# Regrouping the early weight loads of a SwiGLU feed-forward kernel, and the order of its first matmuls

## The chip, the cores and the metric

The kernel runs on one core of one Trainium2 chip. The metric is the device time of one execution in microseconds (us); lower is better. Where one number stands for a kernel it is the median of several executions.

## The reference

All inputs and the output are bf16. There are 2048 tokens, D is 512 and F is 1376.

```python
B, S, D, F = 1, 2048, 512, 1376
def reference(x, w_gate, w_up, w_down):
    g = _silu(x @ w_gate)
    u = x @ w_up
    return (g * u) @ w_down
```

## The kernel before

The kernel computes h = silu(x @ w_gate) * (x @ w_up) with F on the partitions, tile by tile of 128 columns of F, and then multiplies h by w_down. F is 10 full tiles and a rest of 96 columns. The tokens run in 4 chunks of 512 for the first part. For each chunk and F tile there is a *gate* group and an *up* group; a group is 4 matmuls (D is 4 blocks of 128) that add up in one bank of PSUM, 128 x 512 in fp32. ScalarE (ACT) applies silu to the gate's bank and VectorE (DVE) multiplies the result with the up's bank into `hT_sb` (lines 281 and 288). There are 8 banks, used in turn, so groups 0 to 7 (gates and ups of F tiles 0 to 3 of the first chunk: even numbers are gates, odd numbers ups) need no bank to come free. The rest of 96 columns has groups of its own (lines 377 and 388), and the second matrix product follows from line 426 on; the change touches neither.

The engines run without a common clock; each has its own list of instructions, and waits on semaphores. A load has a semaphore of its own that reaches 16 when it has landed, and TensorE (PE) waits for it once, at the first matmul that needs the load (`need`).

*Loads.* Weights are loaded in *slabs*, runs of F tiles, the gates of a slab in one DMA and the ups in another. Each DMA writes 128 partitions with 4 rows each (one for each block of D), a row being 256 bytes per F tile. `slabs` lists the runs as pairs (first tile, tile after the last), and `slab_of` gives the slab's first tile for each tile, which is the name PE waits on. SyncE (SP) issues most loads, in the order written in `loads_on_sync`: token tile 0 (`xn0`), gate 0, then gate and up of tile 1, gates and ups of tiles 2 and 3, two transposing loads of tokens 256 to 383 and 384 to 511 (`x0b`, `x0c`), the two later slabs, the rest of w_up, the other three chunks of x by transposing loads, and w_down. ScalarE's queue issues token tile 1 and up 0 at the start. GpSimd issues no load.

*The start of PE.* PE first runs 10 matmuls on constants (line 338), then transposes the first 256 tokens itself (line 349; DVE and ACT copy the result to `xT_sb`). With these 256 tokens it then runs the first halves (columns 0 to 255) of groups 0 to 7, in an order written out by hand; group 0 in two pieces of 128 columns. Then it runs the second halves in the order of the groups, group 0 again in two pieces, of which the first waits for `x0b` and the second for `x0c`. From group 8 on a group runs over all 512 tokens at once. All these matmuls are issued on line 329, in `gu_matmuls`:

```python
need(("wg" if g["kind"] == "G" else "wu") + str(slab_of[ft]))
```

Of the kernel before, what the change touches and what calls it, by code (L numbers as in the profile page):

```python
# [13 lines left out]
def bass_standalone__swiglu_ffn__prompt_kernel(nc, x, w_gate, w_up, w_down, out):  # L14
# [5 lines left out]
    NFT = NFF + 1  # L20
# [28 lines left out]
    with ExitStack() as es:  # L49
# [32 lines left out]
        def load_sem(name):  # L82
            loads[name] = sem(f"s_{name}")
            return loads[name]
# [6 lines left out]
        def load_x(eng, name, t0, t1):  # L91
            eng.dma_start_transpose(
                xT_sb[:, :, t0:t1], xf[t0:t1, :]
            ).then_inc(load_sem(name), 16)

        def load_w(eng, name, src, base, f0, f1):
            eng.dma_start(  # L97
                w_sb[:, :, base + f0:base + f1],
                src[:, f0:f1].rearrange("(k p) f -> p k f", p=P),
            ).then_inc(load_sem(name), 16)  # L100

        slabs = [(0, 1), (1, 2), (2, 4), (4, 7), (7, NFT)]
        slab_of = {ft: a for a, b in slabs for ft in range(a, b)}

        def load_gate(eng, a, b):
            load_w(eng, f"wg{a}", w_gate, 0, a * P, min(b * P, F))

        def load_up(eng, a, b):
            load_w(eng, f"wu{a}", w_up, UPH, a * P, min(b * P, F - 32))

        def load_xn(eng, i):
            eng.dma_start(xn_sb[:, i, :], xf[i * P:(i + 1) * P, :]).then_inc(load_sem(f"xn{i}"), 16)  # L112
# [5 lines left out]
        def loads_on_sync(sp):  # L118
            load_xn(sp, 0)
            load_gate(sp, *slabs[0])  # L120
            for a, b in slabs[1:3]:
                load_gate(sp, a, b)
                load_up(sp, a, b)
            load_x(sp, "x0b", HT, HT + P)
            load_x(sp, "x0c", HT + P, SC)
            for a, b in slabs[3:]:
                load_gate(sp, a, b)
                load_up(sp, a, b)
            load_w(sp, "wut", w_up, F - (F - 32), F - 32, F)
            for c in range(1, NSC):  # L130
                load_x(sp, f"x{c}", c * SC, (c + 1) * SC)
            sp.dma_start(
                wd_sb[:, 0:NFF, :], w_down[0:NFF * P, :].rearrange("(k p) d -> p k d", p=P)
            ).then_inc(load_sem("wd"), 16)
            load_sem("wdt")
            for y0 in (0, 64):
                sp.dma_start(wd_sb[y0:y0 + 64, T01, :], w_down[NFF * P:F - SR, :]).then_inc(loads["wdt"], 16)
            for x0 in range(0, P, SR):
                sp.dma_start(wd_sb[x0:x0 + SR, T2, :], w_down[F - SR:F, :]).then_inc(loads["wdt"], 16)
            sp.dma_start(wd_sb[0:F_LAST, TAIL, :], w_down[NFF * P:F, :]).then_inc(load_sem("wdl"), 16)  # L140
# [109 lines left out]
        def on_sync(sp):  # L250
            loads_on_sync(sp)
            for t, c0, c1, ob, eng, n in stores:
                sp.wait_ge(s_A if eng == "A" else s_D, n)
                sp.dma_start(of[t * P:(t + 1) * P, c0:c1], o_sb[ob][:, c0:c1]).then_inc(s_out[ob], 16)
            for i in range(NOS):
                sp.wait_ge(s_out[i], 16 * n_store[i])
# [38 lines left out]
        def on_tensor(pe):  # L295
# [19 lines left out]
            def gu_matmuls(g, n0, n1):  # L315
                c, ft = g["c"], g["ft"]
                if c > 0:
                    need(f"x{c}")
                if c == 0 and n1 > HT:
                    need("x0b")  # L320
                if c == 0 and n1 > HT + P:
                    need("x0c")
                need(("wg" if g["kind"] == "G" else "wu") + str(slab_of[ft]))
                col = (0 if g["kind"] == "G" else UPH) + ft * P
                for dk in range(KD):
                    if c == 0 and dk % 2 == 0:
                        for i in range(n0 // P, min(n1 // P, NXN)):
                            after(*xt_ready[i, dk // 2])
                    ins = pe.matmul(  # L329
                        g["bank"][:, n0:n1], lhsT=w_sb[:, dk, col:col + P],  # L330
                        rhs=xT_sb[:, dk, c * SC + n0:c * SC + n1], start=(dk == 0), stop=(dk == KD - 1),
                    )
                if n1 == SC:
                    ins.then_inc(s_P, 1)
# [22 lines left out]
            first = groups[0:NB]  # L357
            for n0, n1 in ((0, P), (P, HT)):
                gu_matmuls(first[0], n0, n1)
            for at in (1, 2, 3, 4, 6, 5, 7):  # L360
                gu_matmuls(first[at], 0, HT)
            for n0, n1 in ((HT, HT + P), (HT + P, SC)):
                gu_matmuls(first[0], n0, n1)
# [108 lines left out]
        on_gpsimd(nc.gpsimd)  # L472
        on_scalar(nc.scalar)
        on_tensor(nc.tensor)
        on_vector(nc.vector)

# [27 lines left out]
```

## Time and profile before

| what | us |
|---|---|
| runs shown | 120.72, 119.93, 120.71 |
| their median | 120.71 |
| the profiled execution, its device time | 120.27 |
| its span, first to last instruction | 119.0 |
| PE busy | 115.6 |
| DVE busy / ACT busy | 37.7 / 34.8 |

The profile is of one execution. PE are the matmuls, PEld the weight loads that go ahead of them, DVE and ACT the vector and the scalar engine, SPq the queue of SP. A line of the chain of work has a start, a length and what ran. A line of the waits names who waited, for whom, the total, the number of waits and the longest. A line of the DMA issues has destination and source, the queue, how many, KB each and the time from issue to landing. A line of a table by stretches has the stretch, its length, then for PE, PEld, DVE, ACT and POOL the busy time and (x) the number of instructions, then the granted clock of PE, the busy share of the DMA engines and what they moved in GB/s. L329 is line 329 of the kernel.

### The profile page before, as it was taken

How to read it: one execution, taken by the hardware profiler on the slowest of the kernel's cores; microseconds unless marked ns; L12 is line 12 of the kernel's file. 1: busy time of each engine (PE TensorE's matmuls, PEld its weight loads, DVE VectorE, ACT ScalarE, POOL GpSimd, SP SyncE). 2: the span in 40 equal slices, each digit the busy share in tenths (PEclk: the TensorE clock that was granted, in tenths of full speed). 3: DMA queues.
4: the chain of work that ended last, by engine and by line, in shares of the span. 5: the costliest groups of instructions: out<-in, count | busy, mean ns of one | idle time of the engine just before them, and what ended most of it. 6: DMA issues, size and time to landing. Idle time of an engine off the chain costs nothing.

```text
span 119.0 us, 2293 instructions
## 1 busy us (share of the span) xinstructions
PE 115.6 (97%) x993; PEld 59.6 (50%) x1001; DVE 37.7 (32%) x57; ACT 34.8 (29%) x60; POOL 1.1 (1%) x7
## 2 busy tenths in 40 slices
PE   7999999999999999999999999999999999999993
PEld 2778444444444444444444444444444445885452
DVE  0105633444434444334444344360000044003320
ACT  4306334362343272442363432430000033003021
POOL 1000000000000000000000000000000000000000
PEclk9999999999999999999999999999999999999999
DMA  2999999992000000000000000000000017200252
GB/s 78 277 190 330 311 165 216 237 357 59 0 6 0 0 0 0 0 0 6 0 0 6 0 0 0 0 0 6 0 6 0 0 59 238 67 0 0 83 187 88
DMA packets 17643, 8.83 MB, mean 74 GB/s; under 512 B 10625, under 2 KB 17633, under 8 KB 17633
## 3 DMA queue, kind: packets, MB, share of 16 engines
q1 hardware_dynamic: 16960, 8.42, 27.5%
q10 hardware_dynamic: 672, 0.26, 0.8%
q8 instruction: 8, 0.13, 0.5%
q14 instruction: 3, 0.02, 0.0%
HBM read 4.75 MB, written 2.10 MB: 58 GB/s over the span
## 4 chain that ended last, share of the span: by engine, by line
PE 92%; DMA 3%; SPq 2%; issue 1%; DVE 0%
PE bank L329 57%; PE bank L426 25%; PE bank L465 7%; DMA w_sb<-in_w_gate_dram 3%; PE bank L377 3%; PE bank L388 2%; SPq L97 1%; SPq L112 0%; DVE o_sb L292 0%
## 5 line engine op out<-in xcount | busy, mean ns | idle before, releaser
L329 PE MATMUL bank<-xT_sb,w_sb 128*128 128x512 bf16 (+2 forms) x355 | 70.0, 355 | 0.4
L329 PEld LDWEIGHTS bank<-xT_sb,w_sb 128*128 128x128 bf16 x360 | 34.2, 98 | 35.3 <-DMA w_sb<-in_w_gate_dram 0.4
L288 DVE TENSOR_TENSOR hT_sb<-sg_sb,bank 128x512 bf16<-128x512 f32 x40 | 27.5, 687 | 40.8 <-PE bank L329 34.5
L281 ACT ACTIVATE sg_sb<-bank 128x512 f32<-128x512 f32 x40 | 23.8, 596 | 41.2 <-PE bank L329 41.2
L426 PE MATMUL bank<-wd_sb,hT_sb 32*128 32x512 bf16 x496 | 29.0, 374 | 0.0
L426 PEld LDWEIGHTS bank<-wd_sb,hT_sb 32*128 32x128 bf16 x496 | 15.3, 93 | 11.5 <-issue 0.4
L292 DVE CAST o_sb<-bank 128x512 bf16<-128x512 f32 (+1 forms) x9 | 5.5, 643 | 31.3 <-PE bank L426 25.9
L281 ACT ACTIVATE o_sb<-bank 128x512 bf16<-128x512 f32 (+1 forms) x8 | 4.3, 582 | 33.6 <-PE bank L426 27.9
L465 PE MATMUL bank<-wd_sb,hT_sb 128*128 128x512 bf16 (+2 forms) x45 | 7.8, 333 | 0.2 <-issue 0.2
L465 PEld LDWEIGHTS bank<-wd_sb,hT_sb 128*128 128x128 bf16 x46 | 4.1, 98 | 4.2 <-issue 0.4
L426 PE MATMUL bank<-wd_sb,hy_sb 32*128 32x512 bf16 (+1 forms) x32 | 5.0, 371 | 0.0
L377 PE MATMUL bank<-xT_sb,w_sb 128*128 128x512 bf16 x14 | 3.8, 379 | 0.1
L288 DVE TENSOR_TENSOR hx_sb<-sgx_sb,bank 32x512 bf16<-32x512 f32 x4 | 2.8, 692 | 3.5 <-ACT sgx_sb L281 3.5
L281 ACT ACTIVATE sgx_sb<-bank 32x512 f32<-32x512 f32 x4 | 2.3, 587 | 4.5 <-PE bank L377 4.5
L338 PE MATMUL bank<-const-bfloat16-1.0 128*128 128x512 bf16 (+1 forms) x10 | 2.8, 466 | 0.8 <-PEq L489 0.8
L426 PE MATMUL bank<-wd_sb,hx_sb 32*128 32x512 bf16 (+1 forms) x16 | 3.0, 371 | 0.0
L377 PEld LDWEIGHTS bank<-xT_sb,w_sb 128*128 128x128 bf16 x16 | 1.6, 98 | 1.9
L281 ACT ACTIVATE sgy_sb<-bank 64x512 f32<-64x512 f32 x4 | 2.4, 590 | 0.1
L338 PEld LDWEIGHTS bank<-const-bfloat16-1.0 128*128 128x128 bf16 x10 | 1.2, 139 | 2.2 <-issue 2.2
L388 PE MATMUL bank<-xT_sb,w_sb 128*64 128x512 bf16 x16 | 1.9, 382 | 0.0
L426 PEld LDWEIGHTS bank<-wd_sb,hy_sb 32*128 32x128 bf16 x32 | 1.6, 93 | 0.6
L292 DVE COPY xT_sb<-bank 128x256 bf16<-128x256 bf16 x2 | 0.6, 292 | 4.1 <-PE bank L349 4.0
(17 smaller groups left out, 8.3 us busy)
## 6 DMA issues: line engine op xcount, KB each, us to landing
out_dram<-o_sb SPq DMA_DIRECT2D x15, 128.0 KB, 1.8
wd_sb<-in_w_down_dram SPq DMA_DIRECT2D x1, 1280.0 KB, 7.4
w_sb<-in_w_gate_dram SPq DMA_DIRECT2D x1, 480.0 KB, 5.4
w_sb<-in_w_up_dram SPq DMA_DIRECT2D x1, 448.0 KB, 6.0
w_sb<-in_w_gate_dram SPq DMA_DIRECT2D x1, 384.0 KB, 3.8
w_sb<-in_w_up_dram SPq DMA_DIRECT2D x1, 384.0 KB, 4.6
w_sb<-in_w_gate_dram SPq DMA_DIRECT2D x2, 128.0 KB, 3.4
w_sb<-in_w_gate_dram SPq DMA_DIRECT2D x1, 256.0 KB, 3.9
```

Of the source, the lines that this page charges most:

```text
L97: eng.dma_start(w_sb[:, :, base + f0:base + f1], src[:, f0:f1].rearrange("(k p) f -> p k f", p=P),).then_inc(load_sem(name), 16)
L281: act.activation(op["out"], op["src"], fn).then_inc(s_A, 1)
L288: ins = dve.tensor_tensor(op["out"], op["a"], op["b"], ALU.mult)
L292: ins = dve.tensor_copy(op["out"], op["src"])
L329: ins = pe.matmul(g["bank"][:, n0:n1], lhsT=w_sb[:, dk, col:col + P], rhs=xT_sb[:, dk, c * SC + n0:c * SC + n1], start=(dk == 0), stop=(dk ...
L338: pe.matmul(banks[NB - 1][:, 0:width], lhsT=ones_w, rhs=ones_m[:, 0:width], start=True, stop=True)
L377: ins = pe.matmul(g["bank"][:, :], lhsT=w_sb[:, dk, XC0:XC0 + P], rhs=xT_sb[:, dk, c * SC:(c + 1) * SC], start=(dk == 0), stop=(dk == KD - 1),
L388: ins = pe.matmul(g["bank"][y0:y1, :], lhsT=w_sb[:, dk, YC0:YC0 + 64], rhs=xT_sb[:, dk, c * SC:(c + 1) * SC], start=(dk == 0), stop=(dk == ...
L426: ins = pe.matmul(g["bank"][:, 0:c1 - c0], lhsT=h, rhs=wd_sb[r0:r0 + SR, w, c0:c1], start=(start and fk == fks[0]), stop=(stop and fk == f ...
L465: ins = pe.matmul(g["bank"][:, 0:c1 - c0], lhsT=h, rhs=w, start=(last and fk == 0), stop=(fk == (NFF if last else NFF - 1)), skip_group_ch ...
```

## The change

Tile 1 and tiles 2 and 3 were two slabs and become one, tiles 1 to 3. Their gates are one load of 384 KB in rows of 768 bytes, and their ups another; before they were a gate load and an up load of 128 KB in rows of 256 bytes, and a gate load and an up load of 256 KB in rows of 512 bytes. SP issues two DMAs less ahead of the two transposing loads. The first halves of the groups run in the order gate 0, up 0, gates 1, 2, 3, ups 1, 2, 3; before it was gate 0, up 0, gate 1, up 1, gates 2, 3, ups 2, 3. The second halves keep their order, and so do all later loads.

```diff
-        slabs = [(0, 1), (1, 2), (2, 4), (4, 7), (7, NFT)]
+        slabs = [(0, 1), (1, 4), (4, 7), (7, NFT)]
...
             load_gate(sp, *slabs[0])
-            for a, b in slabs[1:3]:
-                load_gate(sp, a, b)
-                load_up(sp, a, b)
+            load_gate(sp, *slabs[1])
+            load_up(sp, *slabs[1])
             load_x(sp, "x0b", HT, HT + P)
             load_x(sp, "x0c", HT + P, SC)
-            for a, b in slabs[3:]:
+            for a, b in slabs[2:]:
                 load_gate(sp, a, b)
                 load_up(sp, a, b)
...
-            for at in (1, 2, 3, 4, 6, 5, 7):
+            for at in (1, 2, 4, 6, 3, 5, 7):
                 gu_matmuls(first[at], 0, HT)
```

## The prediction

> **What bounds the kernel now.** I read the page first: span, the busy shares, the slices.
>
> ```profile
> span 119.0 us, 2293 instructions
> PE 115.6 (97%) x993; PEld 59.6 (50%) x1001; DVE 37.7 (32%) x57; ACT 34.8 (29%) x60; POOL 1.1 (1%) x7
> PE   7999999999999999999999999999999999999993
> PE 92%; DMA 3%; SPq 2%; issue 1%; DVE 0%
> ```
>
> The tensor engine is busy for 97% of the span, and the chain that ended last lies on it for 92%. Nothing in the change alters the number or the shape of matmuls, so only the small part of the chain that is not PE can move. Next I read the chain of work in order of time, to find that part.
>
> ```profile
> 1.73 0.50 SPq L97
> 2.27 0.51 SPq L97
> 2.82 3.92 DMA w_sb<-in_w_gate_dram
> 6.74 0.05 issue
> 6.78 5.42 PE bank L329 x52
> ```
>
> Columns: start, length (us), what. The chain runs over the queue of SP into one load, the gates of F tiles 2 and 3, which lands at 2.82 + 3.92 = 6.74 us; from 6.78 on PE runs without a hole. So whatever moves the end of the first 256 tokens moves the end of the kernel by as much. The waits of PE's weight loads before 24 us, the only ones on a DMA:
>
> ```profile
> PEld bank L329 <- DMA w_sb<-in_w_gate_dram: 0.4, 1, 0.4
> PEld bank L329 <- DMA w_sb<-in_w_up_dram: 0.2, 1, 0.2
> ```
>
> Two short waits: up 1 (its weight loads begin at 6.04 us) and gate 2 (at 6.78 us). Last the issues of the DMAs, by narrow stretches, for size and time from issue to landing; the issue times are from the timeline of SP.
>
> ```profile
> 1.26 0.97 SPq L97 DMA_DIRECT2D w_sb<-in_w_gate_dram  x2
> 3.93 2.85 SPq L92 DMA_TRANSPOSE xT_sb<-in_x_dram  x2
> w_sb<-in_w_gate_dram SPq DMA_DIRECT2D x1, 128.0 KB, 3.8
> w_sb<-in_w_up_dram SPq DMA_DIRECT2D x1, 128.0 KB, 3.7
> w_sb<-in_w_gate_dram SPq DMA_DIRECT2D x1, 256.0 KB, 3.9
> w_sb<-in_w_up_dram SPq DMA_DIRECT2D x1, 256.0 KB, 4.2
> w_sb<-in_w_gate_dram SPq DMA_DIRECT2D x1, 384.0 KB, 3.8
> w_sb<-in_w_up_dram SPq DMA_DIRECT2D x1, 384.0 KB, 4.6
> ```
>
> Landings now: gate 1 at 1.73 + 3.8 = 5.53, up 1 at 2.27 + 3.7 = 5.97, gates 2-3 at 6.74, ups 2-3 at 3.37 + 4.2 = 7.57 us. And what the 16 DMA engines moved meanwhile (last column, GB/s):
>
> ```profile
> 3.00:4.00 1.00, 1.00 (x10) 0.80 (x9) 0.00 (x0) 0.23 (x2) 0.00 (x0) 1.00 1.25 287
> 4.50:5.00 0.50, 0.50 (x7) 0.34 (x8) 0.20 (x1) 0.41 (x2) 0.00 (x0) 1.00 0.98 188
> 5.00:5.50 0.50, 0.50 (x8) 0.38 (x6) 0.00 (x0) 0.00 (x0) 0.00 (x0) 1.00 1.11 294
> 5.50:6.75 1.25, 1.16 (x10) 0.62 (x8) 0.00 (x0) 0.00 (x0) 0.00 (x0) 1.00 1.16 340
> 10.00:12.00 2.00, 2.00 (x21) 1.79 (x19) 1.63 (x3) 1.39 (x3) 0.00 (x0) 1.00 1.03 342
> ```
>
> 287 GB/s while rows of 256 bytes are loaded, a dip to 188, then 340 in rows of 512 and 342 in rows of 768 and more.
>
> **The change, part by part.**
>
> *PE's pace.* The 52 matmuls of the chain from 6.78 us are 44 of 256 columns and 8 of 128, as much as 48 of 256: 5.42 us less some 0.16 for the last one's own length (273 ns against its step) is 0.11 us each, 0.44 us for a half group (4 matmuls). Gate 2 to up 3 are four half groups, so the second half of gate 0 starts at 6.78 + 1.76 = 8.54 us. Gate 1 starts at 5.55. Without any wait its six half groups (gates and ups 1 to 3) would end at 5.55 + 2.64 = 8.19. So the waits cost 0.35 us, which is all that can be won (0.3% of the time).
>
> *The waits, new.* The order is now gates 1, 2, 3, ups 1, 2, 3, and the first of them waits for all 384 KB of gates. If these land at L, gate 1 starts at L + 0.04 (as 6.74 to 6.78) and the six half groups end at L + 2.68. That equals 8.54 at L = 5.86. Each 0.1 us of L is 0.1 us of the kernel. What is queued behind: everything of PE, since it runs in order; ScalarE and VectorE have nothing from PE before the second halves (the first silu starts at 9.19 us), and shift with it.
>
> *L from below:* the 384 KB of gates that the kernel loads already took 3.8 us: 1.73 + 3.8 = 5.53, no wait at all. *From above:* by the landing of gates 2-3 now, 6.74, the queue has carried all that the new L needs and up 1 besides. *Between:* gate 1 lands at 5.53 now; 256 KB (262 kB) more at 340 GB/s are 0.77 us, so 6.30. The other way: from 6.74 take up 1's 131 kB, which went at a mean of 241 GB/s (188 and 294), 0.54 us: 6.20; if the dip goes too (half a us at 188 instead of 340: 0.22), 5.98; gate 1 in rows of 768 bytes at 340 instead of 287 saves 0.07: 5.91. The nearest rows give 5.9 to 6.3; I take 6.0, as fewer and larger transfers should do without most of the dip. Gate 1 then starts at 6.04, and the first halves end at 8.68: +0.14 us. A wait of 0.49 us (5.55 to 6.04) at gate 1 stands in the place of the 0.35 lost now.
>
> The Trainium skill (DMA: Bandwidth & Descriptors, Why a DMA increments its semaphore by 16 and not by 1) says that only the full count of 16 means that a load has landed, whatever part is there earlier. The trace agrees: up 1's weight loads start at 6.04, when that load is complete at 5.97, and no earlier. By this rule the merge holds gate 1 back for gates 2 and 3, and the sum is as above; were gate 1 free at its own third, it would start at 5.57 as now and 0.35 us would be won.
>
> *Ups.* Up 1 is needed at 6.04 + 3 x 0.44 = 7.36. Their 384 KB are the last bytes of the same total as now, after the gates: 6.0 + 393 kB / 340 GB/s = 7.16, hidden by 0.2 us. From below 2.27 + 4.6 = 6.87; from above 7.57, the landing of ups 2-3 now, when up 1 starts at 7.61 and the half groups end at 8.93: +0.39 us.
>
> *SP's queue.* Two issues less: 0.51 + 0.52 us and their gaps, 1.1 us, less 0.1 if an issue of 384 KB takes longer (0.58 us against 0.50). So the transposes of tokens 256 to 511 and all later loads are issued 1.0 us earlier. Now the transposes land at 3.93 + 4.3 = 8.23 and 5.52 + 3.1 = 8.62 us and are needed at 8.54 and 8.76: slack 0.31 and 0.14. Their data follows the ups: at the latest they land when they do now, and even a win of 0.35 would want the second at 8.41. Cost nothing at L = 6.0, and they cap a win at 0.14 us should they not come earlier at all. The gates of tiles 4 to 6 land at 6.82 + 3.8 = 10.62 for use at 12.26; covered by more. ACT's and POOL's queues are not touched.
>
> **Sum.** +0.14 us on the profiled execution's 120.27 us (span 119.0 and 1.3 around it): 120.4. The median of the runs shown is 0.44 higher, 120.71, which would give 120.85. The four times known (119.93, 120.27, 120.71, 120.72) have a mean of 120.4, so 120.55; I forecast 120.6.
>
> **Rivals.**
>
> *A, the forecast:* L of 5.8 to 6.4; one wait at gate 1 in place of two; -0.1 to +0.5 us.
>
> *B, the waits go:* gates land at 5.53, as the row of 3.8 us has it; gate 1 starts at 5.57, as now: -0.33 us, about 120.1 (from 120.4). For it: equal total bytes, fewer packets, and one 384 KB load that did take 3.8. Against it: that load had the DMA engines almost free (106 GB/s from 7.50 to 9.00), while this one has four others ahead of it. The Trainium skill (DMA: Bandwidth & Descriptors, Rules for kernel authors and Anatomy of one DMA) advises to coalesce small transfers and fits 2.0 us and bytes / 436e3 to a GpSimd-issued DMA: an estimate of 2.9 us for 384 KB, so a landing at 4.63 and no wait; no row here is as short for one of that size.
>
> *C, slower:* the gates land near 6.74, because the dip stays and the slowest of the 16 engines decides for a longer load: gate 1 starts at up to 6.78, the end moves to 9.42: +0.88 us, 121.3. It decides from L = 6.4 on. For it: the last loads landed 3.8 to 4.2 us after issue whatever their size, and three times the bytes queued at once may cost more. Against it: 131 kB less are ahead.
>
> *D, the ups end last:* +0.39 us at 7.57, 120.8; it needs the ups as late as 7.32 at L = 6.0. For it: the transposes follow directly behind them, as they do behind ups 2-3 now.
>
> *E, the clock:* the first five matmuls of 512 columns took 622 ns each, later ones 379; were PE to fall back to that pace during a wait, the 24 matmuls behind it (2.64 us) would take 622/379 as long, 1.7 us more, over 1% slower. Against it: behind the 0.4 us wait the matmuls still take 273 ns, and the new one is of the same kind.
>
> **How the numbers follow.** Chances: A 0.57, B 0.17, C 0.16, D 0.06, E 0.04. Executions differ by up to 0.8 us, so about 1% (1.2 us) is what a measurement tells from no change. The range reaches to B less some 0.2 of that scatter, 119.9, and to C with as much, 121.5. Faster by over 1% is out of reach of the 0.35 us and left to scatter, 0.03; slower by over 1% needs E or C at its worst with scatter, 0.08; the rest, 0.89, lies within 1%.
>
> **What would show it.** In the waits of PE's weight loads: one on the gate load of about 0.5 us with gate 1's weight loads from about 6.0, none or under 0.1 on the up load, and the long PE piece of the chain from there. A wait on gates under 0.1 is B; over 0.9 is C; one on ups of 0.2 or more is D; matmuls of 256 columns well over 273 ns after the wait are E. The rate from 4.5 to 5.0 us near 340 instead of 188 shows that the dip was one of many small loads. The forecast is wrong if the end of the first halves is not within 8.45 to 9.05 us, or if PE shows a new hole behind it.

## The result, and the profile after

| | before | after |
|---|---|---|
| median, 20 executions each (us) | 120.31 | 120.83 |
| lowest and highest | 119.93, 121.26 | 120.51, 123.48 |
| the profiled execution, device time | 120.27 | 120.63 |
| its span | 119.0 | 119.3 |

The changed kernel is slower: ratio 1.0051, 95% interval 1.0033 to 1.0068, or 0.4 to 0.8 us. The ratio leaves out one execution, of 123.48 with a granted clock of 0.986, the figure of the similar execution e15 below. It is a price of the change all the same: none of the 101 executions of the kernel before, in five batches, took more than 121.26. The changed kernel itself was timed many times in this one batch only.

The page of the changed kernel, the lines that were read first before:

```profile
span 119.3 us, 2299 instructions
PE 115.7 (97%) x1001; PEld 59.6 (50%) x1001; DVE 37.6 (32%) x57; ACT 34.9 (29%) x60; POOL 1.1 (1%) x7
```

PE does what it did; the loss is not in its work. (The traces lack a few matmul records, hence x993 before.) The chain in order of time (start, us, what):

```profile
1.25 4.38 DMA w_sb<-in_w_up_dram
5.62 0.05 issue
5.67 17.21 PE bank L328 x112
```

The waits of PE's weight loads before 24 us, and where the two last of them end (the timeline of PEld; the bracket is the idle time and what ended it):

```profile
PEld bank L328 <- DMA w_sb<-in_w_up_dram: 0.9, 1, 0.9
PEld bank L328 <- DMA w_sb<-in_w_gate_dram: 0.5, 2, 0.3
```

```profile
5.67 0.33 PEld L328 LDWEIGHTS bank<-xT_sb,w_sb 128*128 128x128 bf16 x4 [0.91 <-DMA w_sb<-in_w_up_dram]
6.22 0.11 PEld L328 LDWEIGHTS bank<-xT_sb,w_sb 128*128 128x128 bf16 x2 [0.23 <-DMA w_sb<-in_w_gate_dram]
```

And the DMA issues, up 0 on ACT's queue, the merged gates (issued at 1.73 us) and the merged ups (2.27):

```profile
w_sb<-in_w_up_dram ACTq DMA_DIRECT2D x1, 128.0 KB, 4.4
w_sb<-in_w_gate_dram SPq DMA_DIRECT2D x1, 384.0 KB, 4.5
w_sb<-in_w_up_dram SPq DMA_DIRECT2D x1, 384.0 KB, 5.0
```

Three things are to be seen. The merged gates land at 1.73 + 4.5, in the trace at 6.18 us, and gate 1 starts at 6.22, with L = 6.18 instead of 6.0. Up 0, which the change does not touch, landed at 5.62 instead of 4.50, and PE waited for it; the chain names this wait, since it sees PE as busy from there on. But up 0's half group takes 0.44 us from 5.67, to 6.11, and gate 1 could not start before 6.22 anyway: in this execution the gates decide. The signs that the prediction named did not come as named: it had one wait of about 0.5 us on the gates and under 0.1 on the ups, and here PE waited 0.91 us at up 0 and then 0.23 at gate 1 (the other gate wait of the view is an early one, for gate 0). The merged ups land at 2.27 + 5.0, at 7.24, and nobody waits for them. By the forecast's own rule the six half groups should then end at 6.18 + 2.68 = 8.86, and in the trace the second half of gate 0 starts at 8.858. Before it started at 8.541; the difference, 0.32 us, is that of the spans (119.33 against 119.02).

What the DMA engines moved (last column, GB/s):

```profile
4.50:5.00 0.50, 0.43 (x7) 0.20 (x4) 0.00 (x0) 0.09 (x1) 0.00 (x0) 1.00 1.02 293
5.00:5.50 0.50, 0.00 (x0) 0.00 (x0) 0.00 (x0) 0.00 (x0) 0.00 (x0) 1.00 0.85 260
5.50:6.75 1.25, 1.08 (x9) 0.79 (x10) 0.00 (x0) 0.00 (x0) 0.00 (x0) 1.00 1.26 333
```

The dip to 188 is gone, as expected of larger loads, but 260 and 293 are not 340: another hole stands in its place. What delays the landing shows in the semaphores. The trace has, for each load, the time at which each of the 16 DMA engines reported (us, sorted):

```
before, gate 1         4.71 4.72 4.74 4.75 4.76 4.77 4.79 4.80 4.81 4.82 4.83 4.83 4.85 4.86 4.94 5.50
before, gates 2, 3     5.91 6.02 6.03 6.11 6.16 6.16 6.24 6.24 6.27 6.35 6.35 6.38 6.41 6.41 6.49 6.74
before, up 0           4.25 4.28 4.29 4.31 4.31 4.32 4.34 4.34 4.36 4.36 4.36 4.39 4.40 4.40 4.42 4.50
after,  up 0           3.91 3.97 3.99 4.00 4.01 4.04 4.04 4.07 4.09 4.11 4.35 4.35 4.40 4.41 5.22 5.62
after,  gates 1 to 3   5.08 5.14 5.17 5.18 5.19 5.32 5.32 5.35 5.39 5.57 5.74 5.81 5.96 6.10 6.17 6.18
```

Nine of the 16 engines had the merged gates by 5.4 us; the last needed 0.8 us more. A load has landed when its slowest engine has.

### The profile page after: what moved, and what is told of

It is laid out like the page before. It is cut to its first block, busy times and chain, and to the rows that moved or that the text cites. A ratio compares the mean times of both kernels' runs of the same rounds, so it can differ in the third digit from the quotient of the medians.

```text
span 119.3 us, 2299 instructions
## 1 busy us (share of the span) xinstructions
PE 115.7 (97%) x1001; PEld 59.6 (50%) x1001; DVE 37.6 (32%) x57; ACT 34.9 (29%) x60; POOL 1.1 (1%) x7
## 4 chain that ended last, share of the span: by engine, by line
PE 94%; DMA 4%; ACTq 0%; DVE 0%; issue 0%
PE bank L328 58%; PE bank L425 25%; PE bank L464 7%; DMA w_sb<-in_w_up_dram 4%; PE bank L376 3%; PE bank L387 2%; ACTq L112 0%; DVE o_sb L291 0%
```

## The experiments

All loads and times below are us from the span's start; ratios are to the kernel before, run on the same chip beside each kernel. The theories that the expectations name: **1**, the landing of the merged gates alone sets the loss; **2**, up 0 on ACT's queue is starved by the larger packets on SP's; **3**, the transposing loads, issued 1.1 us earlier, hold up engines; **4**, late engines come with the size of a load; **5**, theory 1 made exact: the start of the second halves follows the last landing that PE waits for, and that is the slowest engine's; **6**, late engines belong to the third load of a queue.

### e1_order_only: the old loads in the new order

```diff
-            for at in (1, 2, 3, 4, 6, 5, 7):
+            for at in (1, 2, 4, 6, 3, 5, 7):
```

> The loads of the kernel before, with the new order of the first halves (gate 0, up 0, gates 1 to 3, ups 1 to 3). Theory 1 (the end of the first halves is set by the landing that the third half group waits for): gate 1 at 5.55 us as before, gate 2 behind its load's landing at 6.74, so from 6.78 five half groups of 0.44 are left instead of four: the second half of gate 0 starts at 8.98 instead of 8.54, +0.44 us, ratio 1.0037. Theory 2 (the changed kernel is slower because up 0, on ACT's queue, is starved by the large packets of the merged gates on SP's queue): the loads are the old ones, so up 0 lands near 4.5 and has no part in it; ratio 1.000 if the order costs nothing by itself. Rival (the order alone is the loss of the changed kernel): ratio 1.005.

Measured: ratio 1.0040, 1.0018 to 1.0062. Theory 1's 1.0037 fits. From the chain:

```profile
2.82 4.54 DMA w_sb<-in_w_gate_dram
7.41 16.22 PE bank L329 x104
```

Gates 2 and 3 landed later here than in the first profile of the same loads (7.37 against 6.74): fifteen engines had them by 6.38, one at 7.37. PE then has five half groups left, 2.2 us, and the second half of gate 0 starts at 9.61. So the new order alone is a loss as long as the loads are the old ones.

### e2_loads_only: the merged loads in the old order

```diff
-            for at in (1, 2, 4, 6, 3, 5, 7):
+            for at in (1, 2, 3, 4, 6, 5, 7):
```

> The merged loads with the old order (gate 1, up 1, gates 2 and 3, ups 2 and 3). Theory 1: gate 1 starts behind the merged gates at 6.22 us, up 1 behind the merged ups, which landed at 7.24 in the changed kernel, so at 7.28; five half groups are left, 2.20: second half of gate 0 at 9.48, +0.94 us on the kernel before, ratio 1.008. Theory 2: up 0 lands at 5.6 or later in this one too, with a wait of 0.7 us or more at up 0, which is hidden by the later waits; the ratio is the same 1.008, or more in the executions where up 0 is later than 6.8.

Measured: 1.0104, 1.0066 to 1.0141. The chain ends its wait at the merged ups, which came 1.0 us later than in the changed kernel's profile; the gates came at 7.16 (thirteen engines by 5.65). Up 0 was whole at 4.60: theory 2's late up 0 did not appear.

```profile
2.27 5.97 DMA w_sb<-in_w_up_dram
8.29 16.22 PE bank L328 x104
```

The two parts of the change thus belong together: each alone costs 0.4% and 1.0%, both together 0.5%.

### e3_up0_on_sync: up 0 taken off ACT's queue

```diff
             load_xn(act, 1)
-            load_up(act, *slabs[0])
...
             load_gate(sp, *slabs[0])
+            load_up(sp, *slabs[0])
             load_gate(sp, *slabs[1])
```

> The changed kernel with up 0 issued on SP's queue behind gate 0 and ahead of the merged gates; ACT's queue issues token tile 1 alone. All later loads on SP are issued about 0.55 us later. Theory 2 (starved by another queue's larger packets): up 0 lands by about 4.9 us all at once, PE does not wait for it, and the scatter of the changed kernel to 121.2 and more goes; time 0.2 us or more below the changed kernel (ratio to the kernel before 1.002 to 1.004). Theory 1 (the landing of the merged gates alone): the gates have the same bytes ahead of them and land at 6.2 as now (same time, 1.005) or 0.5 us later by the later issue (1.009).

Measured: 1.0124, 1.0081 to 1.0167, slower than either theory had it. Against theory 2: up 0, now ahead of the merged gates on the same queue, still had late engines (4.17 to 5.74), and the gates landed at 2.29 + 5.12 = 7.41:

```profile
2.29 5.12 DMA w_sb<-in_w_gate_dram
7.45 16.66 PE bank L328 x108
```

### e4_pairs: tiles 1 and 2 merged, tile 3 alone

```diff
-        slabs = [(0, 1), (1, 2), (2, 4), (4, 7), (7, NFT)]
+        slabs = [(0, 1), (1, 3), (3, 4), (4, 7), (7, NFT)]
...
-            for at in (1, 2, 3, 4, 6, 5, 7):
+            for at in (1, 2, 4, 3, 5, 6, 7):
```

The edit is to the kernel before; its loop over the second and third slab stays.

> Dose between the two kernels: F tiles 1 and 2 merged (gates 256 KB, ups 256 KB, rows of 512 bytes), tile 3 alone; first halves in the order gate 0, up 0, gates 1 and 2, ups 1 and 2, gate 3, up 3. Theory 2: up 0 now competes with packets of 512 bytes and lands between 4.5 and 5.6, about 5.0. Theory 1: 131 kB less are ahead of gate 1's release, so at 340 GB/s it starts about 0.38 us sooner than in the changed kernel, 5.85; the rest follows without a wait of more than 0.1, second half of gate 0 near 8.5; ratio 1.000 to the kernel before. If the issue of four loads in a row binds, the last load (up 3) lands after 7.9 and the ratio is 1.002 or more.

Measured: 1.0004, 0.9984 to 1.0024, no difference from the kernel before in time. In the profiled execution gates 1 and 2 landed at 6.17, fourteen engines by 5.44 and two later; up 0 at 4.49, not at 5.0 as theory 2 would have it.

### e5_after_plain_x and e6_before_plain_x: no transposing loads

```diff
-            load_x(sp, "x0b", HT, HT + P)
-            load_x(sp, "x0c", HT + P, SC)
+            load_plain(sp, "x0b", HT, HT + P)
+            load_plain(sp, "x0c", HT + P, SC)
```

with `load_plain` loading the same bytes without the transpose; tokens 256 to 511 are then computed from data that is not transposed.

> The changed kernel with the two transposing loads of tokens 256 to 511 replaced by plain loads of the same bytes to the same place, so these tokens are computed from data that is not transposed; everything else is as in the changed kernel. Theory 3 (the transposing loads, issued 1.1 us earlier by the change, hold up single DMA engines while up 0 and the merged gates are in flight, and a load lands with its slowest engine): up 0 lands by 4.6 us, the merged gates by 5.5 to 5.8 with all 16 engines within 0.4 us, PE waits less than 0.3 us in all, the second half of gate 0 starts by 8.4, ratio to the kernel before 0.996 to 1.000. Theory 4 (a large load has late engines by its own size, whatever follows it): up 0 after 5 us in some executions, gates at 6.1 or later, ratio 1.004 to 1.006 as the changed kernel.

> The kernel before with the two transposing loads of tokens 256 to 511 replaced by plain loads of the same bytes (these tokens are computed from data that is not transposed). Theory 3: the one late engine of gate 1 (5.50 us where the other fifteen had it by 4.94) is gone, gates 2 and 3 land at 6.5 or earlier, the second half of gate 0 starts at 8.3 or earlier, ratio 0.996 to 0.999. Theory 4: the loads are as in the kernel before, so gates 2 and 3 land at 6.7 and the ratio is 1.000.

Measured: e5 1.0056 (1.0036 to 1.0076), e6 0.9997 (0.9979 to 1.0016). Theory 3 falls: without any transposing load the merged gates had late engines as before (eleven by 5.62, the last at 7.08), gate 1 of e6 too (fourteen by 5.12, then 5.43 and 5.59), and the times are those of the kernels with them.

### e7_wait_gates and e8_wait_gate0: the transposing loads held back

```diff
+            sp.wait_ge(loads["wg1"], 16)      # e8: loads["wg0"]
             load_x(sp, "x0b", HT, HT + P)
```

> The changed kernel in which SP waits for the landing of the merged gates ahead of the two transposing loads, so that none of their work lies beside up 0 and the gates. Theory 3: up 0 by 4.6, gates by 5.5 to 5.8, all 16 engines within 0.4 us; gate 1 starts by 5.8. The transposing loads are issued at about 5.7 instead of 2.8 and land some 4 us later, near 9.7 and 10.3, so that the second half of gate 0 waits about 1.3 us: ratio 1.007 to 1.013. Theory 4: gates at 6.1 or later with late engines, and the rest later still: ratio 1.012 to 1.018.

> The changed kernel in which SP waits for the landing of gate 0 (near 4.2 us) ahead of the two transposing loads, which so are issued about when the kernel before issues them (3.93) or a little later. Theory 3: up 0 is whole by 4.6 us and no wait for it is left; the gates are held up less, landing 5.7 to 6.1; transposing loads land near 8.4 and 8.8; ratio to the kernel before 0.999 to 1.003. Theory 4: as the changed kernel, 1.004 to 1.006, up 0 late in some executions.

Measured: e7 1.0134 (1.0090 to 1.0178), e8 1.0032 (1.0010 to 1.0055). In both the late engines stay: gates at 6.41 in e7, 1.73 + 5.25 = 6.98 in e8. This speaks against theory 3 again, although e8's ratio alone cannot be told from that of the changed kernel, nor from what theory 3 gave it. In e7 up 0 had one engine at 5.48, the other fifteen by 4.37, with nothing on the queues but it and the merged loads.

### e9_up1_on_act and e10_ups_on_act: two queues for the small loads

```diff
             load_up(act, *slabs[0])
+            load_up(act, *slabs[1])           # e10: slabs[2] too
...
-            for a, b in slabs[1:3]:
-                load_gate(sp, a, b)
-                load_up(sp, a, b)
+            load_gate(sp, *slabs[1])
+            load_gate(sp, *slabs[2])
+            load_up(sp, *slabs[2])            # e10: without this line
```

> The kernel before with up 1 issued on ACT's queue behind up 0, so that SP issues gates 2 and 3 about 0.55 us earlier (2.27 us instead of 2.82). Order of the first halves as before. Theory 5 (the start of the second halves follows, one to one, the landing that the last wait stands on, and a landing is that of the slowest of the 16 engines): the earlier issue brings the fifteen quicker engines 0.3 us forward but not the late one surely; second half of gate 0 between 8.2 and 9.2, ratio 0.997 to 1.000, and the span less the start of the second half is 110.5 as in the others. Rival (the issue rate of SP sets the landing of gates 2 and 3): second half of gate 0 at 8.2, ratio 0.996.

> The kernel before with the ups of tiles 1 to 3 issued on ACT's queue (up 0, up 1, ups 2 and 3) and the gates alone on SP's, slabs and order of the first halves as before. The transposing loads are issued 1.1 us earlier, as in the changed kernel, but no load is merged. Theory 5: landings of the single loads as before or up to 0.4 us earlier, less hindered by late engines than a merged load; ratio 0.996 to 1.001. Rival (two queues at once delay the loads that PE needs first, as up 0 in the profile of the changed kernel): gate 1 or up 1 lands after 6.2, ratio 1.003 or more.

Measured: e9 1.0021 (1.0004 to 1.0038), e10 1.0057 (1.0034 to 1.0079); both expected better. In e9's profile gates 2 and 3 landed at 7.07, later than the 6.74 of the first profile although they were issued 0.55 us earlier, so its rival falls. But PE waited for no load there, since it ran at half pace until 6.6 us, and the second half of gate 0 started at 9.10 by that pace. So e9's profile does not show what the landing was worth. The rival of e10 holds: gate 1, a load of 128 KB that is not merged at all, landed at 6.64 (eleven engines by 5.05), up 1 at 7.07, gates 2 and 3 at 8.10. So late engines are no property of merged loads.

### e11_after_again, e15_after_look, e12_before_again, e16_before_look: the two kernels once more

> The changed kernel once more, one look, for the spread of its landings. Theory 5: the merged gates land at L between 6.1 and 7.2 with a gap of over 0.7 us between the first and the last engine; the second half of gate 0 starts at L + 2.68 and the span is 110.5 more. A landing of 6.0 with all engines within 0.4 us would speak against it.

> The kernel before once more, one look. Theory 5: gates 2 and 3 land between 6.7 and 7.4; the second half of gate 0 starts 1.80 us after that landing and the span is 110.5 more.

> The changed kernel once more, one look: L between 6.0 and 7.2, the second half of gate 0 at L + 2.68 and the span 110.5 more.

> The kernel before once more, one look: gates 2 and 3 land between 6.7 and 7.4, the second half of gate 0 starts 1.80 us later, or, where PE is slow until past 6 us and does not wait at all, by its own pace near 9.0; the span is 110.5 more.

Measured: the changed kernel 120.48 and 123.70, the kernel before 120.74 and 120.40. The merged gates landed at 6.04 in e11 (fourteen engines by 5.58), and at 7.67 in e15, where fifteen engines had them by 6.15 and one 1.5 us later. In e15 more happened. From its chain, and then its table by stretches (the last three columns are PE's granted clock, the busy share of the DMA engines, GB/s):

```profile
1.73 5.94 DMA w_sb<-in_w_gate_dram
7.71 18.29 PE bank L328 x108
```

```profile
5.00:7.50 2.50, 0.70 (x7) 0.40 (x6) 0.00 (x0) 0.00 (x0) 0.00 (x0) 1.00 1.95 230
7.75:11.00 3.25, 3.25 (x16) 2.26 (x17) 0.00 (x0) 0.00 (x0) 0.00 (x0) 0.50 0.89 243
11.25:12.00 0.75, 0.75 (x10) 0.67 (x8) 0.00 (x0) 0.00 (x0) 0.00 (x0) 1.00 1.11 377
```

PE waited 2.2 us, and for the next 3.4 us its clock was granted at half: the six half groups took 4.3 us instead of 2.64. The kernel lost 1.5 us to the late engine, against L = 6.18, and 1.6 us more to the clock.

In e12 and e16, the kernel before, PE was not held up by a DMA at all behind the first matmuls. All waits of PE's weight loads before 24 us in e12:

```profile
PEld bank L338 <- issue: 2.2, 6, 0.8
PEld bank L349 <- issue: 0.2, 1, 0.2
```

The matmuls went at half pace until 6.6 us in e12 and 5.9 in e16 (a matmul of 256 columns every 0.21 us instead of 0.11), and the second half of gate 0 started at 9.00 and 8.62.

Across the executions, whatever the kernel, the span less the start of the second half of gate 0 is the same (e4, e5, e6, e9, e10, e13, e14 and e16, not listed, have 110.5 as well):

| execution | last landing waited for | start of second half | span | difference |
|---|---|---|---|---|
| before | 6.74 | 8.54 | 119.02 | 110.5 |
| e12, before | none | 9.00 | 119.48 | 110.5 |
| after | 6.18 | 8.86 | 119.33 | 110.5 |
| e11, after | 6.04 | 8.71 | 119.18 | 110.5 |
| e15, after | 7.67 | 11.98 | 122.45 | 110.5 |
| e1 | 7.37 | 9.61 | 120.09 | 110.5 |
| e2 | 8.24 | 10.48 | 120.96 | 110.5 |
| e3 | 7.41 | 10.08 | 120.56 | 110.5 |
| e8 | 6.98 | 9.66 | 120.14 | 110.5 |

So theory 5 is shown: nothing behind this point differs, and where the clock stays up and PE waits for a load, the point is the landing and 2.68 us (2.24 in e1 and e2, with five half groups left, and 1.80 before, with four). The exception in all runs is e7, where PE waits again for the transposing loads (111.5).

### e13_after_x_on_act and e14_before_x_on_act: another place in the queue

```diff
+            load_xn(act, 0)
             load_xn(act, 1)
...
-            load_xn(sp, 0)
             load_gate(sp, *slabs[0])
```

> The changed kernel with token tile 0 issued on ACT's queue ahead of token tile 1, so that SP issues gate 0 first and the merged gates second, 0.45 us earlier. Theory 6 (late engines belong to the third load of a queue): the merged gates land with all engines within 0.5 us and by 5.6 us; up 0, now third on ACT's queue, is the late one, 5.2 to 6.2; second half of gate 0 at 8.4 to 9.0, ratio 0.998 to 1.003. Theory 4 (late engines by the size of the load): the merged gates keep a gap of 0.8 us or more between first and last engine, L at 5.7 to 6.7, ratio 1.000 to 1.006.

> The kernel before with token tile 0 issued on ACT's queue ahead of token tile 1: SP issues every weight load 0.45 us earlier. Theory 6: gate 1, second on SP's queue, has no late engine, up 1 has one; gates 2 and 3 land near 6.3 and the second half of gate 0 starts near 8.2, unless up 0, third on ACT's queue, comes after 5.6; ratio 0.994 to 0.999. Theory 4: gate 1's engines stay within 0.9 us as in the kernel before, gates 2 and 3 about 0.4 us earlier than before, ratio 0.996 to 1.000.

Measured: e13 1.0208 (1.0181 to 1.0235), e14 1.0018 (0.9996 to 1.0040). The merged gates, now second on SP's queue, came by 5.13 on fifteen engines and at 5.80 on the last: better than the third place, not free of a late engine. Up 0, third on ACT's queue, landed at 1.73 + 5.2, at 6.94, in e13 beside the merged gates, and at 5.40 in e14 beside small loads. The issues of up 0, first e13, then e14:

```profile
w_sb<-in_w_up_dram ACTq DMA_DIRECT2D x1, 128.0 KB, 5.2
```

```profile
w_sb<-in_w_up_dram ACTq DMA_DIRECT2D x1, 128.0 KB, 3.7
```

In e14 gates 2 and 3 landed at 6.26, as theory 6 had it, but PE ran at half pace until 5.8 us, and the second half of gate 0 started at 8.63, not near 8.2.

The pair of up 0 is where theory 2 shows best: the same load in the same place of the same queue takes 1.5 us longer beside the large packets. The Trainium skill (DMA: Bandwidth & Descriptors, Queues, rings and completion order) says that an engine takes packets from its queues in turn. If a packet holds as many rows on one queue as on the other, a queue of 256-byte rows gets a quarter of the bytes beside one of 768, an estimate from that rule. The pair agrees in sign; but with up 0 second on ACT's queue and the merged gates third on SP's it was late in two profiles (5.62 in the changed kernel's, 5.48 in e7) and on time in five (4.45 to 4.63). In e13 PE waited 1.9 us for up 0, and its clock fell for 3.4 us as in e15. The times of all five executions (123.05 to 123.45) suggest that it did so in each; the profile shows it for one.

Theory 6 is half right at best, theory 4 too: the third load of a queue had late engines in most executions, small or large, but not in all (gate 1 of e16 was on all engines by 4.97), and second ones are not always on time.

## Why the prediction was wrong

*That the engines' work does not change and only the first 9 us matter:* right; the 110.5 us behind the second half of gate 0 are the same in every kernel but e7.

*PE's pace and the rule that the six half groups end at L + 2.68:* right to 0.01 us in the profiled execution (8.86) and in e11 (8.71 from 6.04).

*One wait at gate 1 in place of two; ups hidden; SP's queue earlier at no cost:* the one wait was right in e11 and e15, but in the first profile of the changed kernel there were two, at up 0 and gate 1. The merged ups stayed hidden. e5 to e8 show no harm of the earlier transposing loads that is clear of the noise. That up 0, on a queue that the change does not touch, would be held up was not costed; it was the longer wait of that profile, hidden there behind the gates by 0.1 us, and in e13, where it was the last, it cost most of all.

*L:* this is the step that failed. The prediction says "The nearest rows give 5.9 to 6.3; I take 6.0". It was worked out from bytes and mean rates, as if the 16 engines went together. In seven profiles, three of the changed kernel (6.04, 6.18 and 7.67) and four of its variants (6.41, 6.98, 7.08 and 7.16), the merged gates were the third load of SP's queue, and the first engine was done at 5.1 to 5.4 in each: the size of L is that of its slowest engine. Only 6.04 and 6.18 lie within the 5.9 to 6.3; the 6.0 that was taken is about the best case seen, not the usual one. From the medians L can be read backwards: 120.83 less 1.3 around the span, less 110.5 and 2.68, is L = 6.4 us (an estimate; the shortest execution, 120.51, gives 6.0 in the same way), 0.4 above what was taken, and 0.14 + 0.4 is about the 0.52 us between the medians. This takes PE's clock as up by the landing, as in the seven profiles; where it comes up as late as 6.6 us (e12), a part of the 0.4 would be the clock's. Rival C named this mechanism ("the slowest of the 16 engines decides for a longer load") and began at 6.4; the median execution lies on its edge, four of the seven profiles beyond 6.9.

*The sum against the median:* the sum said +0.14 us, but the forecast of 120.6 was put on the mean of four executions and so stood below the median then shown, 120.71. Taken as a change, it pointed to no loss. Adding the sum to the median would have given 120.85; 120.83 was measured. Two errors hid one another there: the kernel before has a median of 120.31 in the 20 executions beside the changed kernel (120.46 to 120.62 in the four later batches). That 120.83 lies so near 120.85 is luck and does not speak for the sum.

*Rival E, the clock:* given 0.04 because "the new one is of the same kind" as the 0.4 us wait. The waits were not: at 2.2 us the clock fell (e15), and it cost 1.6 us, over 1%. The price of 1.7 us was about right, though it came about in another way: matmuls at half pace for 3.4 us.

**What stays open.** Why single engines are late. In the packets of the trace some take 0.2 to 1.3 us instead of 0.02 to 0.04, from about 3.5 to 5.7 us, mostly while a queue's third load is moved. Transposing loads are not the cause, nor is a merged load needed; large packets on the other queue, the place in the queue, the size, and the mere time since the start may each add. Place and time go together in most runs, since the third load is the one then in flight; in e13 the merged gates came second, and their slow packets began at 3.6 us all the same. No run here takes it away, and no version tried was faster than the kernel before.

## What to carry to other kernels

A load that several stages wait for lands when its slowest DMA engine does; cost it by the latest of 16 reports over several executions, not by bytes and a mean rate, and merge only what is needed at one time. Where a forecast is a fraction of a per cent, take the kernel before from more than one execution: with the same loads, gates 2 and 3 landed between 6.56 (e16) and 7.37 us (e1). Where loads are merged, the order of use must follow: e1 and e2 show each half of the change losing by itself.

## What the runs showed of the hardware

- PE's clock fell to half for 3.41 us behind waits of 1.7 (e5), 1.9 (e13) and 2.2 us (e15), each time 3.41 us after it had been raised, and did not fall behind 1.6 us (e2) and 1.4 us (e8). The Trainium skill (TensorE: Matmul & The Clock Gate, HAM oscillation) warns of idle gaps over some 3.4 us; here gaps of half that were enough.
- PE reached full speed between 3.5 us (after) and 6.6 us (e12, by the pace of its matmuls) of the span, with the same ten matmuls ahead. Where it came latest, PE waited for no load (e9, e12) or only for one that landed at 7.37 (e1), and the landings mattered less.
- The load just ahead of a transposing load on its queue mostly reports from all 16 engines at once: 7.47 to 7.53 for ups 2 and 3 before, 7.16 to 7.24 for the merged ups. Exceptions are e15 (one engine at 6.25, the others at 8.65 to 8.72) and e10 (five at 6.40 to 7.26, the others at 7.96 to 8.10). With plain loads behind it (e6), ups 2 and 3 came at 6.85 to 8.00.
